# The low part of each weight block: a subtraction on VectorE, or a DMA that adds

## The chip, the cores and the metric

One core of a Trainium2 chip runs the whole kernel. The metric is the device time of one execution in microseconds (us). The kernel before was timed in three runs: median 1013.14 us, lowest 1011.18, highest 1015.83.

## The reference, cut to what matters

A linear attention with decay makes a matrix x of 3072 tokens by 384 features. Two feed-forward layers follow, and their time is most of the kernel's:

```python
h = x @ w_in                      # 384 x 2048
g = np.where(h > 0, h, np.exp(np.minimum(h, 0)) - 1)
x = g @ w_out                     # 2048 x 384
h = x @ w2_in
g = h * (1 / (1 + np.exp(-1.702 * h)))
out = g @ w2_out
```

The result has to be as exact as float32 products are. The weights arrive as 64-bit floats, seen by the kernel as pairs of 32-bit words.

## The kernel before, in words

**Products in parts.** TensorE multiplies rounded float32 numbers (F32R). So each operand is split into a high part, which is the rounded value, and a low part, which is the value minus the high part. A product is the sum of three matmuls (`PASSES`, L51): high times high, high of the weight times low of the other, low of the weight times high of the other. The third of every group of three is the first that needs the low part of a weight.

**Blocks of weights.** A layer's 2048 hidden features are cut into 16 blocks f of 128. A block is 128 partitions of 768 values: 384 of the first matrix and 384 of the second. The blocks of one layer stay in SBUF, and tokens go through in 6 tiles of 512. Layer 1 is walked tile by tile, and in each tile block by block: 96 steps j of layer 1, then 96 of layer 2.

**How a block is made.** `load_w` (L63) brings the 64-bit words by a DMA from SP. `bits_w` builds the float32 weight t from them in three VectorE instructions (L97 and twice L107). `parts_w` then makes the two parts: ScalarE copies t into the high part with rounding (L132), and VectorE subtracts the high part from t (L133). The tiles t (named wt in the rows) come from a pool with three buffers.

**One step j.** The order of every engine's instructions is the order of this program, written out by hand in `layers` (L537 to L586). TensorE gets the 9 matmuls of h(j) (L143), then the matmuls out(j-2) of the second matrix (L174 in layer 1, L183 in layer 2), with attention's matmuls spread among them. ScalarE and VectorE first split the activations of step j-1 (L166 copies on ScalarE, L167 subtracts on VectorE). Then come the loads, the bits of the next block (L97, L107) and the activation of step j (L154 and L155 on ScalarE, L156 on VectorE; in layer 2 L159 and L160). Behind it come attention's instructions for this step, and then `take("parts", ...)` (L563) with L132 and L133. In the first tile step j makes block f = j + 2, which TensorE wants in step j + 2. Blocks 0 and 1 are made earlier, in the part before step 0 (`lead`, L681). Block 15 is made in step 13.

**Attention beside it.** A chunk of 128 tokens takes four steps, with k = 0 to 3: step j has k = (j + 1) mod 4. In a step with k = 0 VectorE has the masked copies (L375) before L156 and two scans after it (L240, L247). With k = 1 GpSimd has the products kh and r (L270, L278), with k = 2 the state is updated, with k = 3 x is transposed, and GpSimd makes rk and the bonus (L330, L331, L343). L330 and L331 depend on no instruction of the steps before, so GpSimd runs them as soon as its queue reaches them.

**Layer 2.** From step 82 on, the blocks of layer 2 are made at a rate of two in three steps, the parts before the bits (L548 to L558). Blocks 14 and 15 are made in steps 108 and 109 and wanted in steps 110 and 111.

Of the kernel before, what the change touches and what calls it, by code (L numbers as in the profile page):

```python
# [12 lines left out]
F32 = mybir.dt.float32  # L13
# [3 lines left out]
AF = mybir.ActivationFunctionType  # L17
ALU = mybir.AluOpType
# [33 lines left out]
class Moe:  # L52
# [75 lines left out]
    def parts_w(self, layer, f):  # L128
        nc = self.nc
        t = self.t.pop((layer, f))  # L130
        w = self.w[layer, f] = self.p["w"].tile([P, 2, 2 * DM], F32R, tag=f"w{f}", name=f"w{f}")
        nc.scalar.copy(w[:, 0, :], t)  # L132
        nc.vector.tensor_tensor(out=w[:, 1, :], in0=t, in1=w[:, 0, :].bitcast(F32), op=ALU.subtract)  # L133

    def h(self, layer, f, x, n):

# [751 lines left out]
```

## Time and profile before

| what | value |
|---|---|
| median of 3 runs | 1013.14 us |
| the profiled execution: device time, span | 1009.45 us, 1007.2 us |
| TensorE (PE) busy | 966.6 us, 96% |
| weight load (PEld) busy | 829.3 us, 82% |
| VectorE (DVE) busy | 707.3 us, 70% |
| ScalarE (ACT) busy | 459.6 us, 46% |
| GpSimd (POOL) busy | 179.5 us, 18% |
| DMA queues | one queue of SP's with 100.98 MB, none of GpSimd's |

The span runs from the first to the last instruction; the time holds what lies around it too. Busy shares are means over stages with different limits: in the 40 slices of the profile VectorE is at 9 tenths in the first tenth of the span and at 6 to 7 in the middle, TensorE at 7 to 8 at first and at 9 after the sixth slice. Rows name an instruction's engine, its line in the kernel, its operation and "output<-inputs" with buffer numbers left out.

### The profile page before, as it was taken

How to read it: one execution, taken by the hardware profiler on the slowest of the kernel's cores; microseconds unless marked ns; L12 is line 12 of the kernel's file. 1: busy time of each engine (PE TensorE's matmuls, PEld its weight loads, DVE VectorE, ACT ScalarE, POOL GpSimd, SP SyncE). 2: the span in 40 equal slices, each digit the busy share in tenths (PEclk: the TensorE clock that was granted, in tenths of full speed). 3: DMA queues.
4: the chain of work that ended last, by engine and by line, in shares of the span. 5: the costliest groups of instructions: out<-in, count | busy, mean ns of one | idle time of the engine just before them, and what ended most of it. 6: DMA issues, size and time to landing. Idle time of an engine off the chain costs nothing.

```text
span 1007.2 us, 13002 instructions
## 1 busy us (share of the span) xinstructions
PE 966.6 (96%) x4895; PEld 829.3 (82%) x4895; DVE 707.3 (70%) x1102; ACT 459.6 (46%) x886; POOL 179.5 (18%) x147
## 2 busy tenths in 40 slices
PE   7888889999999999999999999999999999999997
PEld 5677677788888878878888879999989899899896
DVE  7999997677667766776635888757666676676432
ACT  3243344444444445444445554446565565544322
POOL 5542323333323423423300000000000000000000
PEclk9798989999999999999999999999999999999999
DMA  9845401221211222212005560134353354432001
GB/s 239 231 176 177 146 28 51 86 72 52 83 51 51 61 83 71 74 45 90 1 1 193 195 216 25 41 119 135 122 181 123 119 180 124 142 116 79 32 1 35
DMA packets 35351, 101.89 MB, mean 101 GB/s; under 512 B 4048, under 2 KB 7248, under 8 KB 35280
## 3 DMA queue, kind: packets, MB, share of 16 engines
q1 hardware_dynamic: 35280, 100.98, 31.4%
q8 instruction: 40, 0.66, 0.3%
q14 instruction: 31, 0.25, 0.1%
HBM read 91.53 MB, written 9.44 MB: 100 GB/s over the span
## 4 chain that ended last, share of the span: by engine, by line
PE 78%; DVE 14%; issue 3%; POOL 2%; ACT 1%; DMA 0%; ACTq 0%; POOLq 0%; DVEq 0%
PE h L143 34%; PE o L183 20%; PE o L174 16%; DVE wt L107 4%; PE py L450 3%; PE pa L450 2%; DVE w L133 2%; DVE hl L167 1%; DVE wt L97 1%; DVE g L156 1%; PE pd L450 1%; DVE parts L294 1%; DVE e L240 1%; DVE gi L247 1%; ACT w L132 1%
## 5 line engine op out<-in xcount | busy, mean ns | idle before, releaser
L143 PE MATMUL h<-xt,w 128*128 128x512 f32 x1728 | 469.4, 401 | 4.2 <-DVE w L133 3.0
L143 PEld LDWEIGHTS h<-xt,w 128*128 128x128 f32 x1728 | 318.1, 189 | 66.5 <-DVE w L133 5.8
L174 PE MATMUL o<-hl,w 128*128 128x512 f32 x864 | 280.5, 428 | 6.1 <-DVE x L515 6.1
L183 PE MATMUL o<-w,hl 128*128 128x384 f32 x1152 | 217.8, 337 | 3.1 <-ACT e L159 2.1
L183 PEld LDWEIGHTS o<-w,hl 128*128 128x128 f32 x1152 | 204.4, 188 | 13.0 <-ACT e L159 3.3
L166 ACT CAST hl<-g 128x512 fp32r<-128x512 f32 x192 | 118.9, 619 | 188.4 <-DVE g L156 86.0
L174 PEld LDWEIGHTS o<-hl,w 128*128 128x128 f32 x864 | 158.5, 193 | 32.5 <-DVE x L515 7.5
L167 DVE TENSOR_TENSOR hl<-g,hl 128x512 fp32r<-128x512 f32 x192 | 150.2, 783 | 43.7 <-ACT hl L166 42.4
L156 DVE SCALAR_TENSOR_TENSOR g<-e,h 128x512 f32<-128x512 f32 x96 | 65.6, 683 | 68.1 <-ACT e L155 67.7
L160 DVE TENSOR_TENSOR g<-e,h 128x512 f32<-128x512 f32 x96 | 65.9, 686 | 66.5 <-ACT e L159 66.5
L159 ACT ACTIVATE e<-h 128x512 f32<-128x512 f32 x96 | 57.3, 597 | 101.0 <-PE h L143 101.0
L154 ACT ACTIVATE e<-h 128x512 f32<-128x512 f32 x96 | 57.3, 596 | 54.2 <-PE h L143 54.0
L450 PEld LDWEIGHTS py<-tok,at 128*128 128x128 f32 x304 | 60.4, 200 | 15.7 <-issue 4.4
L107 DVE SCALAR_TENSOR_TENSOR wt<-raw,wt 128x768 int32<-128x768 int32 x64 | 67.5, 1055 | 1.6
L155 ACT ACTIVATE e<-e 128x512 f32<-128x512 f32 x96 | 60.7, 632 | 3.1
L375 DVE COPY_PREDICATED at<-mask,pa 128x512 f32<-128x512 int32 x48 | 32.3, 726 | 38.6 <-PE pa L450 38.5
L270 POOL TENSOR_TENSOR kh<-kr,gi 112x512 f32<-112x512 f32 x19 | 31.6, 1661 | 150.1 <-issue 133.0
L450 PE MATMUL py<-tok,at 128*128 128x48 f32 x304 | 50.3, 248 | 6.2 <-issue 3.6
L450 PE MATMUL pa<-parts,khl 112*128 112x256 f32 x192 | 54.5, 284 | 1.0 <-DVE parts L294 1.0
L123 DVE TENSOR_SCALAR checked<-checked 128x384 f32<-128x384 f32 x64 | 22.8, 356 | 39.7 <-ACT checked L122 39.7
L378 ACT COPY kt<-pk 128x448 f32<-128x448 f32 x20 | 10.7, 534 | 86.2 <-PE pk L450 64.0
L132 ACT CAST w<-wt 128x768 fp32r<-128x768 f32 x32 | 26.7, 833 | 49.5 <-DVE wt L107 44.5
(111 smaller groups left out, 933.4 us busy)
## 6 DMA issues: line engine op xcount, KB each, us to landing
raw<-in_w SPq DMA_DIRECT2D x32, 768.0 KB, 4.5
seen<-in_w SPq DMA_DIRECT2D x64, 384.0 KB, 3.2
tok<-in_tok SPq DMA_DIRECT2D x20, 576.0 KB, 3.9
kr<-in_rkw SPq DMA_DIRECT2D x20, 448.0 KB, 3.6
seen<-in_rkw SPq DMA_DIRECT2D x24, 226.2 KB, 3.6
x2d<-x SPq DMA_DIRECT2D x18, 256.0 KB, 2.3
x<-x2d SPq DMA_DIRECT2D x18, 256.0 KB, 3.8
w<-in_rkw SPq DMA_DIRECT2D x20, 226.2 KB, 2.6
```

The costliest lines, as they stand in the source:

```text
L107: yield nc.vector.scalar_tensor_tensor(out=ti, in0=a, scalar=n, in1=ti, op0=shift, op1=put)
L143: nc.tensor.matmul(h[:, :n], w[:, a, k * P:(k + 1) * P], x[:, b, k, :n], start=i == 0, stop=i == len(mm) - 1)
L154: nc.scalar.activation(e[:, :n], h[:, :n], AF.Exp)
L155: nc.scalar.activation(e[:, :n], e[:, :n], AF.Relu, bias=1.0, scale=-1.0)
L156: nc.vector.scalar_tensor_tensor(out=g[:, :n], in0=e[:, :n], scalar=-1.0, in1=h[:, :n], op0=ALU.mult, op1=ALU.max)
L159: nc.scalar.activation(e[:, :n], h[:, :n], AF.Sigmoid, scale=1.702)
L160: nc.vector.tensor_tensor(out=g[:, :n], in0=e[:, :n], in1=h[:, :n], op=ALU.mult)
L166: nc.scalar.copy(hl[:, 0, :n], g[:, :n])
L167: nc.vector.tensor_tensor(out=hl[:, 1, :n], in0=g[:, :n], in1=hl[:, 0, :n].bitcast(F32), op=ALU.subtract)
L174: nc.tensor.matmul(acc[d][:, :n], w[:, a, DM + d * P:DM + (d + 1) * P], hl[:, b, :n], start=f == 0 and i == 0, stop=f == NF - 1 and i == 2)
L183: nc.tensor.matmul(acc[s][:, :DM], hl[:, b, s * P:(s + 1) * P], w[:, a, DM:2 * DM], start=f == 0 and i == 0, stop=f == NF - 1 and i == 2)
L450: b[done]()
```

## The change

The high part is made as before. ScalarE then writes the negated high part to where the low part is to stand, and a DMA that GpSimd issues adds t to it. VectorE has no part in it any more.

```diff
         nc.scalar.copy(w[:, 0, :], t)
-        nc.vector.tensor_tensor(out=w[:, 1, :], in0=t, in1=w[:, 0, :].bitcast(F32), op=ALU.subtract)
+        nc.scalar.activation(w[:, 1, :], w[:, 0, :].bitcast(F32), AF.Copy, scale=-1.0)
+        nc.gpsimd.dma_start(w[:, 1, :].bitcast(F32), t, accum_op=ALU.add)
```

## Rows read from the trace of the kernel before

**Rows 1.** Busy time by stretch: stretch, length, PE, PEld, DVE, ACT, POOL, clock, DMA.
```profile
80.00:88.00 8.00, 8.00 (x36) 7.14 (x35) 7.82 (x11) 1.75 (x3) 4.15 (x3) 0.61 0.40 144
88.00:96.00 8.00, 7.90 (x36) 6.13 (x36) 7.90 (x9) 2.48 (x4) 2.24 (x2) 0.97 1.00 330
...
600.00:700.00 100.00, 99.09 (x498) 89.65 (x497) 73.77 (x114) 48.26 (x99) 0.00 (x0) 1.00 0.26 86
```

**Rows 2.** Groups by line and form: count, busy us, mean ns, idle before.
```profile
L133 DVE TENSOR_TENSOR w<-wt,w 128x768 fp32r<-128x768 f32 x32 | 30.5, 954 | 1.2 <-ACT w L132 0.3
...
L132 ACT CAST w<-wt 128x768 fp32r<-128x768 f32 x32 | 26.7, 833 | 49.5 <-DVE wt L107 44.5 <-DMA tok<-in_tok 2.5 <-DMA raw<-in_w 2.5
...
L97 DVE TENSOR_SCALAR wt<-raw 128x768 int32<-128x768 int32 x32 | 21.3, 664 | 0.0
```

**Rows 3.** L133 between 44 and 160 us, and who waited for it (us, times).
```profile
L133 DVE TENSOR_TENSOR w<-wt,w x16: 929/950/959, 46.1 to 157.5; 128x768 fp32r<-128x768 f32 x16
...
  PEld h L143: 5.8, 7
```

**Rows 4.** Timeline of steps 5 to 7, all engines: start, us, instruction, wait before.
```profile
96.04 0.68 DVE L156 SCALAR_TENSOR_TENSOR g<-e,h 128x512 f32<-128x512 f32 x1
96.16 0.84 ACT L132 CAST w<-wt 128x768 fp32r<-128x768 f32 x1 [2.48 <-DVE wt L107]
...
96.89 0.62 ACT L166 CAST hl<-g 128x512 fp32r<-128x512 f32 x1
...
98.39 0.68 DVE L167 TENSOR_TENSOR hl<-g,hl 128x512 fp32r<-128x512 f32 x1
...
98.53 0.73 PE L143 MATMUL h<-xt,w 128*128 128x512 f32 x2 [0.21 <-DVE w L133]
...
105.81 0.63 ACT L155 ACTIVATE e<-e 128x512 f32<-128x512 f32 x1
...
108.76 0.68 DVE L156 SCALAR_TENSOR_TENSOR g<-e,h 128x512 f32<-128x512 f32 x1
```

**Rows 5.** Timeline of VectorE, from step 4 to step 13.
```profile
87.80 3.33 DVE L107 SCALAR_TENSOR_TENSOR wt<-raw,wt 128x768 int32<-128x768 int32 x2
91.06 0.67 DVE L156 SCALAR_TENSOR_TENSOR g<-e,h 128x512 f32<-128x512 f32 x1
...
92.99 0.68 DVE L167 TENSOR_TENSOR hl<-g,hl 128x512 fp32r<-128x512 f32 x1
...
94.17 1.95 DVE L107 SCALAR_TENSOR_TENSOR wt<-raw,wt 128x768 int32<-128x768 int32 x2
...
124.61 0.68 DVE L156 SCALAR_TENSOR_TENSOR g<-e,h 128x512 f32<-128x512 f32 x1
...
138.19 0.68 DVE L156 SCALAR_TENSOR_TENSOR g<-e,h 128x512 f32<-128x512 f32 x1
...
153.61 0.67 DVE L156 SCALAR_TENSOR_TENSOR g<-e,h 128x512 f32<-128x512 f32 x1
```

**Rows 6.** Timeline of GpSimd (POOL) in step 4.
```profile
87.31 1.31 POOL L330 TENSOR_TENSOR rk<-tok 128x384 f32<-128x384 f32 x1
88.70 1.62 POOL L331 TENSOR_TENSOR rk<-rk,u 128x384 f32<-128x384 f32 x1
```

**Rows 7.** Timeline of TensorE (PE) where block 15 is wanted.
```profile
158.51 0.50 PE L143 MATMUL h<-xt,w 128*128 128x512 f32 x1 [0.61 <-DVE w L133]
```

**Rows 8.** DMA issues: output<-input, queue, count, KB each, median us from issue to landing.
```profile
raw<-in_w SPq DMA_DIRECT2D x32, 768.0 KB, 4.5
seen<-in_w SPq DMA_DIRECT2D x64, 384.0 KB, 3.2
...
lent<-in_tok SPq DMA_DIRECT2D x4, 576.0 KB, 15.1
```

**Rows 9.** Timeline of steps 108 and 110, block 14 of layer 2.
```profile
643.76 0.83 ACT L132 CAST w<-wt 128x768 fp32r<-128x768 f32 x1
...
648.90 2.24 PE L143 MATMUL h<-xt,w 128*128 128x512 f32 x9
```

## The prediction

> **What bounds the kernel now.** I read the page first: TensorE is busy for 96% of the span, VectorE for 70%. That says nothing of single stages, so the busy time by stretch comes next. Between 88 and 96 us both engines are nearly full (7.90 of 8 us), while between 600 and 700 us TensorE has 99.09 of 100 and VectorE only 73.77 [rows 1]. So there are two stages. While the first tile runs beside the making of layer 1's blocks (to about 158 us) VectorE sets the pace. Later TensorE does, and nothing taken from VectorE there shortens anything. The groups by line give the size of what goes: 32 subtractions of 954 ns, 30.5 us [rows 2]. Who waits for them comes from the view of L133: 16 of them lie between 46.1 and 157.5 us, and the weight load of h stood waiting behind seven of these, 5.8 us in all [rows 3]. The reader is to see two things there: only 16 x 0.954 = 15.3 us can be on the path, and the low part has no slack. TensorE wants it at the moment it is ready, already now. The chain through the first tile and the timeline of steps 5 to 13 (S(j) below is the start of L156 in step j) show what follows what.
>
> **Removed: VectorE's time.** Less of it comes back than 0.95 us per block, since L167, the next on VectorE, waits for L166, and L166 now stands on ScalarE behind the negation. In step 5, L132 starts 0.12 us after S, L166 starts 0.73 behind L132 and takes 0.62; L167 starts 2.35 after S [rows 4]. A negation of the shape of L132 (833 ns busy [rows 2], the next start 0.73 later) puts the end of L166 at 0.12 + 0.73 + 0.73 + 0.62 = 2.2, and L167 at about 2.25. So the step with k = 2 and no state to update gets 0.1 back. The step with k = 1 (step 4) had L167 at 92.99 - 91.06 = 1.93 [rows 5] and loses 0.3. With k = 3 the same count gives 0.14 back, with k = 2 and a state to update 0.7 to 0.9. Only in steps with k = 0, where the scans give ScalarE time, does nearly all come back (0.88). Over the 14 steps 0 to 13 that is 4.4 us. The two subtractions in the lead give 1.9.
>
> **Moved: GpSimd's queue.** The DMA waits for the negation, and GpSimd waits with it. Behind it stand L330 and L331. They now run in step 4 beside both L107, which take 3.33 us there and 1.95 a step later [rows 5, 6]. In the new order they stand behind the DMAs of blocks 6 and 7, so that the L107 of step 4 lose the company: 1.4 us back, and 1.4 again in step 8. They then run beside L97 and L107 of step 6, where the next term decides. Who waits for L331 is the sum q in step 6, about 1 us after S(6); the DMA of block 7 leaves GpSimd about 2.7 after S(5), and 2.9 us of L330 and L331 behind it end in time. kh and r stand behind the DMA of block 5, whose negation is done before the scans that kh needs: nothing.
>
> **Added: the DMA's landing.** Call L the time from the end of the negation until TensorE is released. The trace has no DMA of GpSimd's and none that adds. The nearest rows: 384 KB, just this size, land 3.2 us after SP's issue, 768 KB after 4.5 [rows 8]. The addition reads two sources of 384 KB, so I take the 768 KB row, 4.5, and for GpSimd's part in issuing about 1.0, below its shortest product in [rows 6]: L = 5.5. The low end is 3.2 (only that size moved); the far end is 15.1, loads queued behind each other [rows 8].
>
> By the Trainium skill, "DMA: Bandwidth & Descriptors", section "Anatomy of one DMA", a DMA issued by GpSimd takes about 2.0 us plus its bytes at 436 GB/s, an estimate of 2.9 us here; the 3.2 of SP's row agrees with that, and no run here shows one of GpSimd's. With it the landing would be hidden, which is the first rival.
>
> The low part is there at S + 0.12 + 0.73 + 0.83 = S + 1.7, plus L. Where this reaches VectorE is to be seen in the period from S(5) to S(9). The third matmul of h(7) starts at 98.53, when it is released by L133; the exponentials of step 7 end at 105.81 + 0.63 = 106.44, which is 7.9 us later, with the scores' matmuls and a copy (L378) between. S(7) is 108.76 [rows 4]. So S(7) can't come before S(5) + 1.7 + 5.5 + 7.9 = 15.1, and came after 12.7: 2.4 late. From S(7) to S(9) VectorE's path holds again and gives back 0.88 + 1.4 - 0.3 = 2.0. The period costs 0.4. From S(9) to S(11) it was 138.19 - 124.61 = 13.6 [rows 5], by the same sum 15.1, 1.5 late; to S(13) come back 0.88 - 0.3 and about 0.5 where L330 leaves the second L107 alone: again 0.4.
>
> The other terms. Start, S(5): the lead gives 1.9; blocks 1 and 2 land among four loads of 768 KB, which costs about 1.0 of it; S(3) is late by about 1.6 as in the other periods, and steps 3 and 4 give back 2.0: together -1.3. Blocks 6 and 10 land while loads fill the DMA engines (share 1.00 between 88 and 96 [rows 1]): about 1 us later each, half of which passes the slack of h(6) and h(10): +1.0. Block 15: the low part came at 158.46, S(13) + 4.85, as the third matmul of h(15) starts at 158.51 [rows 5, 7]; now it comes at S(13) + 7.2. TensorE has nothing to do meanwhile: +2.35. From there on TensorE is the bound, and a delay stays.
>
> Layer 2: ScalarE's 16 negations stand before the activation there, which has about 2 us of slack until VectorE takes it up, behind L107: nothing, and 13 us if that cover were gone. But block 14 is copied at 643.76 and would land at 643.76 + 1.6 + 5.5 = 650.8, and h(110), begun at 648.90, wants it with its third matmul at about 649.4 [rows 9]: +1.5. Block 15 comes 4.9 us later and is wanted 4.2 later, so it hides behind that wait but for 0.7, which VectorE's lighter queue covers. Earlier blocks have a step more.
>
> **Sum.** -1.3 + 0.4 + 0.4 + 1.0 + 2.35 + 1.5 = +4.35 us on the profiled 1009.45. The median of the runs is 3.7 above that execution, so 1013.14 + 4.35 = 1017.5. The slope is 5 us of time per us of L (S(3), S(7), S(11), block 15, layer 2), and L = 4.6 would be no change.
>
> **Rivals.** *The landing is hidden.* With L = 3.2, S(7) and S(11) go by VectorE's path but for 0.3 each: 4.4 + 1.9 + 2.8 = 9.1 back, less about 1: 1005. For it speaks the row of equal size; against it the seven waits for a low part that came 3 us earlier. *The landing is long.* If the addition or GpSimd's issue takes 2.5 us more (L = 8), five places pay: +12.5, 1030. This is the rival on the other side of no change, and it decides from L = 4.6 on; 0.5% is passed at L = 5.65. For it: GpSimd's products are the slowest in the trace, and loads queued at full DMA share took 15.1 [rows 8]; against it: the DMA engines are mostly free after 96 us. *The clock falls.* In step 4 TensorE was granted 0.61 for 8.0 us [rows 1], 1.2 GHz for most of it, after steps in which it had waited for low parts [rows 3]; new waits make more of that. At the full 2.4 GHz that work would take 4.9, so three more such steps cost 9.3 on top: 1027. *GpSimd is held off by VectorE.* L107 beside GpSimd's products slows to 1.7 times [rows 5], so the two engines do get in each other's way. If an L97 (664 ns [rows 2]) holds up each issue at the four places up to block 15, that adds 2.7: 1020. By the Trainium skill, "SBUF — State Buffer", section "Who interferes with whom", GpSimd can't write a DMA's descriptors while a VectorE instruction uses both ports, and it advises against hiding such a DMA under VectorE. By that rule this last rival holds; no row here has such a DMA.
>
> **How the numbers follow.** Forecast 0.47 (its own range 1011 to 1022), hidden landing 0.13, long landing 0.26, clock 0.06, held off 0.08. A measurement of this kernel can tell 0.5%, about 5.1 us, from no change. The hidden landing is faster (0.13). The forecast lies under the bound by 0.7 us, so its chance goes to the same for 0.31 and to slower for 0.16; long landing, clock and most of held off are slower too. That makes faster 0.13, same 0.34, slower 0.53. The range goes from the hidden landing, 1005, to a little above the long one, 1031.
>
> **What would show it.** Right: no L133; a GpSimd queue with 32 DMAs of 384 KB, landing about 5 us after issue; before the third matmul of h(3), h(6), h(7), h(11), h(15) waits of 2 to 5 us for a DMA; L167 waiting for L166 in steps with k = 1; VectorE with visible idle time between 60 and 158 us; a wait before h(110). Wrong: TensorE's waits no longer than now, with S(13) before 150 (faster than forecast), or landings of 8 us and more, or a clock under 0.9 in stretches where it was 1.00, or a loss that arises after 165 us, where I count 1.5.

## The result, and the profile after

The changed kernel takes 1027.07 us (median; 1023.53 to 1027.77) where the kernel before took 1012.16 beside it: ratio 1.0134 [1.0098, 1.0169]. It is slower by about 14 us. The profiled execution took 1023.53 us, its span is 1021.5 against 1007.2. Two executions of runs further down are left out of the ratios: one of the ten without loads took 1886.46 us, and the profiled one of its control 1991.71 us, with a mean of 713 ns for each matmul of h where the kernel before has 401, which no run explains.

The page of the changed kernel has VectorE's 25 us less, ScalarE's 27 more and a second DMA queue. Lines after L133 have moved on by one: L133 is now the negation, L134 the DMA, L144 the product h, L157 the instruction that was L156.

```profile
PE 966.6 (95%) x4895; PEld 830.2 (81%) x4895; DVE 682.2 (67%) x1070; ACT 486.8 (48%) x918; POOL 200.7 (20%) x179
...
q0 software_dynamic: 4608, 12.58, 6.6%
...
L144 PE MATMUL h<-xt,w 128*128 128x512 f32 x1728 | 476.7, 405 | 27.1 <-DMA w<-wt 27.1
L144 PEld LDWEIGHTS h<-xt,w 128*128 128x128 f32 x1728 | 321.3, 191 | 90.4 <-DMA w<-wt 30.6
...
L134 POOL DMA_DIRECT2D w<-wt x32 | 28.2, 882 | 190.0 <-ACT w L133 105.1
...
raw<-in_w SPq DMA_DIRECT2D x32, 768.0 KB, 7.0
seen<-in_w SPq DMA_DIRECT2D x64, 384.0 KB, 3.2
w<-wt POOLq DMA_DIRECT2D x32, 384.0 KB, 5.3
```

TensorE is busy for the same 966.6 us and now stands 27.1 us before h for the new DMA. (The weight load's 30.6 are the same waits seen from the other row; they are not added.) The last three rows answer to [rows 8]: the loads of raw words, with which the change has nothing to do, have gone from 4.5 to 7.0 us, and the 384 KB of the added DMA land in 5.3, while SP's transfer of that size stays at 3.2. So the new DMA and the loads of raw words hold each other up. Most of what the loads lose is in layer 2 (median 4.3 us before, 6.3 after, between 540 and 700 us); in the first tile they were slow already (6.9, now 7.5). No engine waits for a load of raw words between 40 and 190 us of the changed kernel, so it is not the later loads that cost the time there.

Where the waits lie is asked of L134 in the first tile, 44 to 178 us. Its rows "PEld h" and "PE h" say how long TensorE's weight load and matmul of h waited for it, in us and times:

```profile
L134 POOL DMA_DIRECT2D w<-wt x16: 854/871/1160, 46.1 to 165.7; - x16
...
  PEld h L144: 30.6, 8
  PE h L144: 27.1, 8
...
DMA to landing us min/median/max: 3.8/5.0/9.2
```

In the kernel before, the weight load waited 5.8 us for the subtraction [rows 3], and the matmul less:

```profile
  PE h L143: 3.0, 6
```

All of the waiting for the DMA is in the first tile: between 560 and 700 us, where layer 2's blocks are made, no engine waits for w<-wt, though its landings take 3.7 to 8.8 us there too. The landing varies from 3.8 to 9.2, and two waits make most of the total. The timeline of SP, GpSimd and TensorE shows them (start, us, instruction, wait before it):

```profile
53.88 1.52 SPq L63 DMA_DIRECT2D raw<-in_w  x3
...
56.15 0.40 SPq L63 DMA_DIRECT2D raw<-in_w  x1
...
56.99 0.88 POOL L134 DMA_DIRECT2D w<-wt  x1 [1.29 <-ACT w L133]
...
66.24 0.80 PE L144 MATMUL h<-xt,w 128*128 128x512 f32 x1 [6.63 <-DMA w<-wt]
...
89.60 0.91 SPq L63 DMA_DIRECT2D raw<-in_w  x2
...
92.83 0.43 SPq L63 DMA_DIRECT2D raw<-in_w  x1
...
95.70 0.66 SPq L63 DMA_DIRECT2D raw<-in_w  x1
...
96.29 0.87 POOL L134 DMA_DIRECT2D w<-wt  x1 [3.86 <-ACT w L133]
...
105.28 2.93 PE L144 MATMUL h<-xt,w 128*128 128x512 f32 x6 [8.44 <-DMA w<-wt]
...
164.23 2.93 PE L144 MATMUL h<-xt,w 128*128 128x512 f32 x6 [2.96 <-DMA w<-wt]
```

Block 1, issued at 56.99, releases TensorE 9.2 us later; block 6, issued at 96.29, 9.0 later. SP issued four loads of raw words of 768 KB from 53.88 to 56.15, and four more from 89.60 to 95.70: both DMAs were issued less than 1 us behind the last load of such a group. Those two waits are 15.1 of the 27.1 us. The other six share 12.0, none above 3.0.

Busy time by stretch (columns as in [rows 1]) at those two places, and at the end of the tile:

```profile
62.00:66.00 4.00, 0.00 (x0) 0.00 (x0) 2.91 (x4) 0.00 (x0) 0.46 (x1) 0.79 1.04 300
66.00:70.00 4.00, 3.76 (x12) 3.20 (x13) 0.00 (x0) 0.00 (x0) 0.00 (x0) 0.50 1.04 321
...
98.00:102.00 4.00, 0.00 (x0) 0.00 (x0) 3.04 (x6) 2.18 (x3) 0.27 (x1) 0.98 1.03 353
102.00:106.00 4.00, 0.72 (x2) 0.63 (x3) 3.97 (x3) 0.00 (x0) 2.94 (x3) 0.50 1.05 271
...
161.00:165.00 4.00, 1.04 (x4) 0.67 (x3) 3.92 (x6) 2.62 (x5) 1.55 (x1) 0.79 1.02 229
165.00:169.00 4.00, 4.00 (x13) 2.92 (x11) 3.87 (x5) 2.10 (x4) 3.17 (x3) 0.50 0.52 103
```

TensorE is empty, or nearly so, while the DMA engines are full, and in the stretch in which it starts again its granted clock is 0.50, 1.2 GHz. In 160 to 195 us that is a cost of its own: the mean clock there was 1.00 before (TensorE busy for 33.12 us of 35) and is 0.90 now (30.16). From 40 to 160 us it is 0.90 against 0.91, since the kernel before had its own stretch of 0.61 [rows 1].

The steps' starts, in the timeline of VectorE, answer to [rows 4, 5] for steps 5, 7, 9, 11 and 13:

```profile
99.61 0.68 DVE L157 SCALAR_TENSOR_TENSOR g<-e,h 128x512 f32<-128x512 f32 x1
...
119.04 0.69 DVE L157 SCALAR_TENSOR_TENSOR g<-e,h 128x512 f32<-128x512 f32 x1 [1.30 <-ACT e L156]
...
132.93 0.68 DVE L157 SCALAR_TENSOR_TENSOR g<-e,h 128x512 f32<-128x512 f32 x1
...
148.78 0.69 DVE L157 SCALAR_TENSOR_TENSOR g<-e,h 128x512 f32<-128x512 f32 x1 [1.19 <-ACT e L156]
...
163.64 0.67 DVE L157 SCALAR_TENSOR_TENSOR g<-e,h 128x512 f32<-128x512 f32 x1
```

The first tile's end is seen in the first store of its output (view of the tile x2d; in the kernel before that row begins at 177.1):

```profile
L517 SPq DMA_DIRECT2D x2d<-x x18: 326/344/1200, 190.3 to 614.8; - x18
```

Of 14.3 us in the span, 13.2 have arisen by 190 us. An estimate from stretches of 2 us says what they are: from 46 us to the first store TensorE is idle for 28.0 us, before for 14.7, and its busy time at less than the full clock loses 11.8 us, before 9.9. So the waits make nearly all of it and the clock about 2 us.

### The profile page after: what moved, and what is told of

Its sections match the earlier page's. It is cut to its first block, busy times and chain, and to the rows that moved or that the text cites. A ratio compares the mean times of both kernels' runs of the same rounds, so it can differ in the third digit from the quotient of the medians.

```text
span 1021.5 us, 13131 instructions
## 1 busy us (share of the span) xinstructions
PE 966.6 (95%) x4895; PEld 830.2 (81%) x4895; DVE 682.2 (67%) x1070; ACT 486.8 (48%) x918; POOL 200.7 (20%) x179
## 4 chain that ended last, share of the span: by engine, by line
PE 80%; DVE 7%; DMA 6%; ACT 4%; issue 3%; POOL 0%; SPq 0%; ACTq 0%; DVEq 0%; POOLq 0%
PE h L144 35%; PE o L184 20%; PE o L175 16%; DMA w<-wt 3%; PE py L451 3%; PE pa L451 3%; DMA lent<-in_rkw 1%; DVE wt L107 1%; PE pd L451 1%; ACT w L132 1%; ACT w L133 1%; DVE g L157 1%; DVE wt L97 1%; DVE parts L295 1%; DMA u<-in_u 1%
## 5 line engine op out<-in xcount | busy, mean ns | idle before, releaser
L144 PE MATMUL h<-xt,w 128*128 128x512 f32 x1728 | 476.7, 405 | 27.1 <-DMA w<-wt 27.1
L144 PEld LDWEIGHTS h<-xt,w 128*128 128x128 f32 x1728 | 321.3, 191 | 90.4 <-DMA w<-wt 30.6
L175 PE MATMUL o<-hl,w 128*128 128x512 f32 x864 | 276.7, 424 | 6.1 <-DVE x L516 6.1
L167 ACT CAST hl<-g 128x512 fp32r<-128x512 f32 x192 | 118.7, 618 | 163.3 <-DVE g L157 78.8
L168 DVE TENSOR_TENSOR hl<-g,hl 128x512 fp32r<-128x512 f32 x192 | 148.6, 774 | 54.1 <-ACT hl L167 52.9
L157 DVE SCALAR_TENSOR_TENSOR g<-e,h 128x512 f32<-128x512 f32 x96 | 65.7, 684 | 85.9 <-ACT e L156 85.3
L134 POOL DMA_DIRECT2D w<-wt x32 | 28.2, 882 | 190.0 <-ACT w L133 105.1
L451 PEld LDWEIGHTS py<-tok,at 128*128 128x128 f32 x304 | 57.7, 190 | 7.9
L156 ACT ACTIVATE e<-e 128x512 f32<-128x512 f32 x96 | 60.7, 632 | 3.0
L451 PE MATMUL py<-tok,at 128*128 128x48 f32 x304 | 48.1, 239 | 0.0
```

What stands on the lines that cost most here:

```text
L144: nc.tensor.matmul(h[:, :n], w[:, a, k * P:(k + 1) * P], x[:, b, k, :n], start=i == 0, stop=i == len(mm) - 1)
L156: nc.scalar.activation(e[:, :n], e[:, :n], AF.Relu, bias=1.0, scale=-1.0)
L157: nc.vector.scalar_tensor_tensor(out=g[:, :n], in0=e[:, :n], scalar=-1.0, in1=h[:, :n], op0=ALU.mult, op1=ALU.max)
L167: nc.scalar.copy(hl[:, 0, :n], g[:, :n])
L168: nc.vector.tensor_tensor(out=hl[:, 1, :n], in0=g[:, :n], in1=hl[:, 0, :n].bitcast(F32), op=ALU.subtract)
L175: nc.tensor.matmul(acc[d][:, :n], w[:, a, DM + d * P:DM + (d + 1) * P], hl[:, b, :n], start=f == 0 and i == 0, stop=f == NF - 1 and i == 2)
```

## The experiments

The theory: the added DMA is harmless where the DMA engines are free, and costs TensorE 5 to 8 us where it is issued behind a group of SP's loads of raw words. The rivals: ScalarE's negation costs the time; the addition makes the DMA slow; GpSimd's way of issuing does; or a few us are lost at every block. Letters in the expectations are those that each expectation explains. Each diff is against the changed kernel, except where it says otherwise.

**Layer 2 alone.** Layer 1's blocks are made as before. (The two lines without a sign are the changed kernel's, moved under the condition.)

```diff
+        if layer == 2:
             nc.scalar.activation(w[:, 1, :], w[:, 0, :].bitcast(F32), AF.Copy, scale=-1.0)
             nc.gpsimd.dma_start(w[:, 1, :].bitcast(F32), t, accum_op=ALU.add)
+        else:
+            nc.vector.tensor_tensor(out=w[:, 1, :], in0=t, in1=w[:, 0, :].bitcast(F32), op=ALU.subtract)
```

> The negation and the adding DMA are used for the 16 blocks of layer 2 alone; layer 1's blocks are subtracted on VectorE as before. Theory A (the whole loss arises in the first tile, where TensorE waits for landings behind SP's loads): 1012 us, ratio 1.000 +- 0.003, no wait of TensorE for the DMA. Theory of the prediction (block 14 of layer 2 lands too late): 1.5 us more, 1013.7. Rival (the loss is spread over both layers): 1016 or more.

Measured: 1013.68 us against 1012.01, ratio 1.0024 [1.0005, 1.0042]. Half of the negations and DMAs, with all that they take from ScalarE and GpSimd in layer 2, cost 0.05 to 0.4%. So most of the loss needs layer 1's blocks, which are made in the first tile. The 1.7 us left are near the 1.5 that the prediction gave to block 14 of layer 2, but no engine waits for w<-wt in this run's trace either, so they do not show that term.

**The negation alone.** ScalarE negates as in the change, VectorE then subtracts over it as before.

```diff
-        nc.gpsimd.dma_start(w[:, 1, :].bitcast(F32), t, accum_op=ALU.add)
+        nc.vector.tensor_tensor(out=w[:, 1, :], in0=t, in1=w[:, 0, :].bitcast(F32), op=ALU.subtract)
```

> ScalarE writes the negated high part as in the changed kernel, and VectorE then subtracts over it as in the kernel before; no DMA. Theory A: the negation is a small part: L133 has to wait for it, 0.65 us in each of four steps with k = 1 and 0.2 in six others, about 4 us, 1016. Rival C (ScalarE's longer queue is what costs the time): 1022 or more, near the changed kernel's 1027.

Measured: 1029.59 us, ratio 1.0175 [1.0141, 1.0210]: a miss, and not a clean test. The subtraction overwrites the negation, so VectorE has to wait for ScalarE's second pass as well; in the kernel before it waited for the first one once, 0.3 us [rows 2]. The waits between 560 and 690 us (who, for whom: us, times, longest) have it:

```profile
DVE w L134 <- ACT w L133: 14.7, 16, 0.9
```

TensorE falls to 92.92 us in 600 to 700, where it had 99.09 [rows 1], and 8.3 us are gone by the first store (185.4). So it does not tell the negation's own price from that of the added wait; it says that the two together are not covered in either stage.

**The DMA without its addition.** A copy of t takes the addition's place, so the low part is not the low part.

```diff
-        nc.gpsimd.dma_start(w[:, 1, :].bitcast(F32), t, accum_op=ALU.add)
+        nc.gpsimd.dma_start(w[:, 1, :].bitcast(F32), t)
```

> The DMA copies t over the negated high part and doesn't add, so the low part is t itself; bytes read fall from two sources to one. Theory A (the landing is long only because SP's loads fill the DMA engines): the landings of blocks 1, 6 and 10 stay above 6 us, those in quiet stretches come down from 4 us by less than 1; time 1020 to 1025. Rival B (the addition itself is slow): landings near 3 us everywhere, time 1013 or less.

Measured: 1021.46 us, ratio 1.0095 [1.0062, 1.0129]. The landings go down to 2.5 us in quiet stretches but are still 6 to 8 behind the loads (blocks 1, 2, 6 and 10), and TensorE waits 25.4 us in place of 27.1:

```profile
  PEld h L144: 28.4, 7
  PE h L144: 25.4, 7
...
DMA to landing us min/median/max: 2.5/3.2/7.8
```

The addition adds 1.3 us to the shortest landing and some 4 us to the time (1.0134 against 1.0095, with intervals that overlap); most of the loss is there without it.

**The loads away.** Nine loads of raw words of layer 1 are left out; blocks 5 to 13 are made from the words of block 14, loaded early. Every negation and DMA stays.

```diff
+        if layer == 1 and 5 < f < 15:
+            self.raw[1, f] = self.raw["one"]
+            return
+        s = 14 if (layer, f) == (1, 5) else f
...
+        if s != f:
+            self.raw["one"] = self.raw[1, f]
-        self.nc.sync.dma_start(raw, src[f])
+        self.nc.sync.dma_start(raw, src[s])
```

> The changed kernel without nine of the loads of layer 1's weights: blocks 5 to 13 are built from block 14's words, loaded in place of block 5's. Everything else runs as it does. Theory A: blocks 6 and 10 land within 4.5 us of issue, block 1 (beside the first loads, of which three of four are gone) within 6; the waits of 9, 9 and 7 us fall to 5 or less, and the time to 1008 to 1015. Rivals B, C and D (a slow addition, ScalarE's queue, GpSimd held off by VectorE) don't depend on the loads: 1022 or more.

Measured: 1012.65 us, ratio 1.0012 [0.9986, 1.0037]. No loss can be told any more. The view of its DMA between 40 and 180 us:

```profile
  PEld h L150: 23.3, 10
  PE h L150: 18.9, 10
...
DMA to landing us min/median/max: 3.8/4.0/6.2
```

TensorE still waits 18.9 us for the DMA, none longer than 4.8, and yet the time is that of the kernel before. The reading is that what VectorE is spared pays for the quiet landings, and only the long ones are left over.

**The control.** The same edit of the loads on the kernel before.

> The control to the run without loads: the kernel before, with the same nine loads of layer 1's weights left out (blocks 5 to 13 built from block 14's words). Theory A: the kernel before hardly waits for loads (one 2.5 us wait of ScalarE behind raw), so 1009 to 1012. If it gets faster by 10 us or more, the loads cost every kernel time, and the run without loads told nothing of landings.

Measured: 1010.50 us, ratio 0.9985 [0.9964, 1.0006]. Its only trace is of the execution of 1991.71 us, so its times alone are used. The loads by themselves cost the kernel before nothing that can be measured; beside the DMAs they cost 14 us.

**The negation on GpSimd.**

```diff
-        nc.scalar.activation(w[:, 1, :], w[:, 0, :].bitcast(F32), AF.Copy, scale=-1.0)
+        nc.gpsimd.tensor_scalar(out=w[:, 1, :], in0=w[:, 0, :].bitcast(F32), scalar1=-1.0, scalar2=None, op0=ALU.mult)
```

> The changed kernel with the negation on GpSimd instead of ScalarE. Theory A: the landings stay as they are (a little later by GpSimd's slower pass, 0.2 to 1 us), so 1027 to 1033. Rival C (ScalarE's longer queue is a large part): 1020 or less.

Measured: 1032.73 us, ratio 1.0215 [1.0173, 1.0257]. ScalarE has none of the change's work any more and the loss is larger. Between 40 and 170 us TensorE waits for the DMA much as before:

```profile
PEld h L144 <- DMA w<-wt: 29.6, 9, 7.8
PE h L144 <- DMA w<-wt: 25.8, 8, 7.4
```

So the loss does not need ScalarE's longer queue. It is no clean price of it, since GpSimd takes 2.3 us for each negation where ScalarE takes 0.85; the run without loads, which keeps all 32 negations on ScalarE and loses nothing, says the same more directly.

**Another issuer.** The plain copy again, issued by ScalarE, through its hardware queue.

```diff
-        nc.gpsimd.dma_start(w[:, 1, :].bitcast(F32), t, accum_op=ALU.add)
+        nc.scalar.dma_start(w[:, 1, :].bitcast(F32), t)
```

> The plain copy (no addition) issued by ScalarE's hardware queue in place of GpSimd's. Theory A (the DMA engines are full of loads, whoever issues): blocks 1, 6 and 10 land 5 us or more after issue as in the plain copy from GpSimd, time 1018 to 1025. Rival D (GpSimd's own descriptor making is what is late): all land within 3.5 us, 1014 or less.

Measured: 1029.23 us, ratio 1.0155 [1.0114, 1.0196], outside what was expected. It is to be held against GpSimd's plain copy. The landings are as there, 2.5 to 7.6 us, the long ones again behind the loads, and TensorE waits as long in the first tile:

```profile
  PEld h L144: 27.1, 6
  PE h L144: 24.7, 5
...
DMA to landing us min/median/max: 2.5/2.7/7.6
```

GpSimd's way of issuing is therefore not the cause of the long landings. Most of what this run loses beyond GpSimd's plain copy lies behind the first tile: the first store comes at 192.7 us against 190.7, and from there to the end of the span it takes 837.4 against 829.8. In 600 to 640 us, in layer 2, TensorE has 36.32 us where the plain copy has 39.03. ScalarE issues from the queue in which its activations stand; that this is the reason was not tested.

**Four DMAs, far from the loads.** Blocks 0, 5, 9 and 13 of layer 1 by the DMA, all else by VectorE.

```diff
+        if layer == 1 and f in (0, 5, 9, 13):
             nc.scalar.activation(w[:, 1, :], w[:, 0, :].bitcast(F32), AF.Copy, scale=-1.0)
             nc.gpsimd.dma_start(w[:, 1, :].bitcast(F32), t, accum_op=ALU.add)
+        else:
+            nc.vector.tensor_tensor(out=w[:, 1, :], in0=t, in1=w[:, 0, :].bitcast(F32), op=ALU.subtract)
```

> The negation and the adding DMA for blocks 0, 5, 9 and 13 of layer 1 only (the steps with k = 0, and the one in the lead), where the low part is wanted late and no load of weights runs; all others subtracted on VectorE. Theory A (the landing costs only where TensorE wants the block at once or loads are in the way): no wait of TensorE for a DMA, and 0.95 + 3 x 0.88 = 3.6 us back, 1008.5, ratio 0.9965. Rival C (ScalarE's queue): the gain is eaten, 1012 or more.

Measured: 1008.39 us against 1010.86, ratio 0.9953 [0.9932, 0.9973]: a little faster than both kernels. TensorE's waits for the DMA and for VectorE's subtractions between 40 and 175 us:

```profile
PEld h L147 <- DVE w L137: 4.8, 6, 1.7
...
PE h L147 <- DVE w L137: 2.4, 4, 1.3
...
PEld h L147 <- DMA w<-wt: 0.9, 1, 0.9
...
PE h L147 <- DMA w<-wt: 0.4, 1, 0.4
```

**All but the blocks behind the loads.** As the last, with ten blocks of layer 1 by the DMA: all but 1, 2, 6, 10, 14 and 15.

```diff
+        if layer == 1 and f not in (1, 2, 6, 10, 14, 15):
```

> The low parts of blocks 0, 3, 4, 5, 7, 8, 9, 11, 12 and 13 of layer 1 by the DMA; those of blocks 1, 2, 6, 10, 14 and 15, whose DMAs were issued among the loads of later blocks or at the end of the tile, and all of layer 2 by VectorE. All loads stay. Theory A (the loss is the landing beside the loads): the landings take 3.8 to 5.3 us from issue, TensorE waits for a DMA at most some 5 us in all, and the time is 1008 to 1014 us, ratio about 0.998. Rival B (a few us are lost at every block made by a DMA): ten of 32 blocks lose about a third to a half of the 14 us, 1016 to 1019 us. Rival C (mixing makers costs by itself, since a block of VectorE queues behind another's): the DMA waits are gone and the time is yet above 1016 us.

Measured: 1010.73 us against 1011.86, ratio 0.9981 [0.9958, 1.0005]. All loads are there, ten of 16 DMAs too, and the loss is gone. The expected 5 us of waiting was too little:

```profile
PEld h L147 <- DMA w<-wt: 16.0, 6, 4.5
...
PE h L147 <- DMA w<-wt: 13.4, 6, 4.1
```

In the view of the DMA's line no landing is long:

```profile
DMA to landing us min/median/max: 3.8/4.1/5.1
```

Still TensorE waits 13.4 us for them, as in the run without loads; by the same reading VectorE's relief pays for that. The two runs take the collision away from its two sides, once the loads and once the DMAs, and both end at the time before. That is as far as "shown" goes. This run is the less pure of the two, since VectorE here subtracts blocks 14 and 15 and all of layer 2 as well, which do not collide with loads of the first tile. That a loss of a few us at every block adds up to the 14 is refuted by the same two runs, with 16 and 10 DMAs in the first tile.

## Why the prediction came out as it did

It forecast 1017.5 us, slower by less than can be told from no change; it became 1027.07, inside the range and on the side that had the largest chance, but 9.6 us above the forecast, with a loss three times as large as the sum's 4.35. That it lies in the range is owed to the long landing, a rival that set the upper end and did not come as it was put. The mechanism held in its outline: the low part has no slack in the first tile, and the time that VectorE saves (busy for 96.09 us between 40 and 160, before for 116.66) is handed over to waits of TensorE's for the landing. L167 waits for L166 as foreseen (now L168 for L167, 8.3 us in nine times between 40 and 190). But two of the prediction's own signs of being wrong came up as well: landings of 8 us and more, and a clock under 0.9 where it was 1.00. The step that failed is one term of the sum: "blocks 1 and 2 land among four loads of 768 KB, which costs about 1.0", and its twin "Blocks 6 and 10 land while loads fill the DMA engines: about 1 us later each, half of which passes". These were sized at 2.0 us together. Step by step, from the starts above and [rows 4, 5]:

| stretch | forecast | measured |
|---|---|---|
| up to S(5) | -1.3 | 99.61 - 96.04 = +3.6 |
| S(5) to S(9) | +0.4, and +0.5 for block 6 | 33.32 - 28.57 = +4.75 |
| S(9) to S(13) | +0.4, and +0.5 for block 10 | 30.71 - 29.00 = +1.7 |
| S(13) to the first store | +2.35 | 26.7 - 23.5 = +3.2 |
| the rest of the span | +1.5 | 831.2 - 830.1 = +1.1 |
| sum | +4.35 | +14.3 |

- *The landing beside loads.* The first two rows are 4.9 and 3.85 us over, 8.75 of the 9.95 that the sum was short. They hold block 1 and block 6, which landed 5.4 and 5.1 us later than a quiet one (3.8). A row that warned of it stood in [rows 8]: loads queued behind each other took 15.1 us. It was used as the far end for all landings alike, and no price for the few issued behind loads was taken from it.
- *The quiet landing, L.* 5.5 from the end of the negation was too much: 3.8 to 4.1 from issue, and the issue follows the negation's end by 0.3 us where GpSimd waits for it (96.29 behind 95.15 + 0.85), so L is 4.1 to 4.4. The forecast's slope, 5 us per us of L with no change at 4.6, gives 1.0 to 2.5 us faster for that; neither run without the collision shows a change that could be told, 1.0012 and 0.9981.
- *The five places.* Waits were named before h(3), h(6), h(7), h(11) and h(15). They came before h(1), h(3), h(4), h(6), h(9), h(10), h(13) and h(14). The count of steps with and without slack was too fine for the way in which one delay shifts the next.
- *Block 15.* Its size was nearly right for a wrong reason: TensorE waited 2.96 us for block 14, then worked at 1.2 GHz for 4 us (165 to 169), and block 15 landed behind that unseen.
- *Layer 2.* No wait came. Block 14's low part would have been late by the old order of things [rows 9], but VectorE, with 954 ns less per block, makes the blocks sooner: block 14's negation starts at 655.50 and h(110) at 662.11. That 1.1 us are left there, near the 1.5 of the sum, is chance and not told apart: single executions of the kernels whose layer 2 is as before show 830 to 834 us for that stretch (the four and the ten blocks).
- *The rivals.* The hidden landing fell at block 1, which held TensorE for 6.63 us. The long landing came near in time (1030) but not as it was put: not every landing is long; four in the first tile are (blocks 1, 2, 6 and 10: 9.2, 8.3, 8.9 and 6.9 us). The clock is a part, not the cause: some 2 us, by the estimate above, and as many by the stretch of 165 to 169 us alone (4 us at half). GpSimd was not held off: its DMA instructions took 854 to 1160 ns, median 871, with VectorE busy beside them. The rule of the Trainium skill that stood behind this rival ("SBUF — State Buffer", section "Who interferes with whom") is not seen at work here.

## What to carry to other kernels

A DMA that takes over work from a busy engine is priced by what stands in the DMA engines when it is issued, and not by its bytes alone: look for loads issued in the us before it, and give the landing of those few transfers a longer price of its own (here 9 us, where a quiet one took 4). Take such a DMA only for tiles whose issue falls into a quiet stretch; here four of 32 gained 0.5%, where all 32 lost 1.3%. And a wait that only replaces another wait (18.9 us of it in the run without loads) may cost nothing, so compare when the stage ends, not the sum of the waits.

## What the runs showed of the hardware

An accumulating DMA of 384 KB, issued by GpSimd, lands in 3.8 to 4.1 us at best (blocks 0, 3, 4, 8, 12 and 15), a plain one of the same blocks in 2.5 to 3.1. How the queues share the engines behind a group of loads was the surprise. These are the DMA queues' rows (packets, MB, share of 16 engines) for block 6, issued at 96.29, first in 98 to 100 us, then in 102 to 104:

```profile
q1 hardware_dynamic: 168, 0.81, 99.8%
```

```profile
q0 software_dynamic: 68, 0.21, 53.5%
q1 hardware_dynamic: 66, 0.40, 50.5%
```

From issue to 100 us GpSimd's queue (q0) moved not one packet; its first came between 100.5 and 101, and from then on it had half of the engines. In a quiet stretch (issue at 113.09) 33 of its 144 packets have moved by 115, the first after 114.4. So the delay of 5.1 us has two parts: a start that is about 3 us late, and half the rate, about 2 us. The Trainium skill, "DMA: Bandwidth & Descriptors", section "Queues, rings and completion order", says that each DMA engine takes turns between the queues that have work, a packet at a time. The second part agrees with that. By that rule alone the 144 packets, which take about 2.1 us in the quiet stretch (41.0% of 113 to 118 us), would have taken 2.1 more and landed 5.9 us from issue (an estimate); measured were 8.9. What holds the first packet back is not seen in the trace, and since the copy on ScalarE's hardware queue was as late (7.6 us), it is not GpSimd alone; it stays open.
